# Moving two of the seven products: the fourth product of a Bu group goes up two places, and the first output group takes its second product before its fifth

## The chip, the cores and the metric

The kernel runs on one core of one Trainium2 chip. Its time is device microseconds from one execution of the whole program; a kernel is judged by the median of several executions. TensorE is called PE below, VectorE is DVE, ScalarE is ACT, GpSimd is POOL, and SyncE, which only issues transfers here, is SP.

## What is computed

The input x has 2048 rows (time) of 1024 columns. Two branches read it, and a gate per row mixes them:

```python
g = _sigmoid((x * gate_w).sum(-1, keepdims=True))
a = _A_ref(x, ...)        # Bu = x @ B_bar^T;  h[t] = Lam_bar * h[t-1] + Bu[t];  y = 2 Re(h @ C^T) + x * Dskip
b = _B_ref(x, ...)        # layernorm(x) -> @ w1 + b1 -> gelu -> @ w2 + b2
return g * a + (1 - g) * b
```

Branch a is a linear recurrence with 1024 complex states, branch b an MLP with 3584 hidden columns. Everything comes and goes in bf16.

## The kernel before, in words

**The matrix products.** Nearly all are done in groups of a 2 by 2 block product with seven multiplications instead of eight (Strassen in Winograd's form). Class `SG` writes one group: the methods `p1` to `p7` each put one accumulated product of 128 by 512 on PE (function `mm`, line 869 for the first product in a PSUM bank and line 871 for those that add to what stands there). A group uses three of the eight banks. Bank a gets p1, ACT copies it to bank b (the "seed", line 904), then p2 adds to a, and quadrant 0 is read out of a (`fin(0)`). Bank e gets p5, ACT saves it ("s5", line 888), then p3 adds to it and quadrant 1 is read out (`fin(1)`). Bank b starts with the seed; p6 adds to it and ACT saves it ("su", line 888 or 889); p7 adds, quadrant 3 is read out (`fin(3)`); p4 adds, quadrant 2 is read out (`fin(2)`). So p4 may start only when the read of quadrant 3 is over, p3 only after s5, p6 and p2 only after the seed.

**The stages**, in the order of PE: transposes and eight plain products; 14 groups of Bu (`bu_group`, four matmuls a product); then blocks of MLP groups, first layer (`m_group`, four matmuls a product) and second layer (`b_group`, seven), four of each, alternating; then eight output groups (`y_group`, eight matmuls a product). The second layer of half 1 adds its results to a DRAM buffer scr_ac by accumulating transfers from POOL's queue (line 1414); the output stage loads them back (line 1479). The recurrence itself (`ssm`: scans of line 1212, products of lines 1198 and 1201) runs on DVE beside all of this, at the lowest priority.

**The order of PE** is written out by hand: `mm` makes each product depend on the one before it. In a Bu group it is p1, p7 of the group before, p5, p6, p2, p3, p4 of the group before. At the passage from the last second-layer group (called b1.3 below) to the first output group (y0) it is p7 of b1.3, p1 of y0, p5 of y0, p4 of b1.3, p6, p2, p3 of y0, then p1 of y1 and so on.

**The order of the other engines** comes from a list planner (`Graph._schedule_once`): it plays the program through with costs that are constants of the file, and whenever an engine falls free it gives it the ready operation with the smallest priority; among equal priorities the one that was created first. Waits are then added, and each engine runs its list strictly in that order. A priority is a pair: a stage number and the running number of a product, less or more a few places.

**What reads out a Bu group.** `fin(0)` and `fin(2)` are ACT copies (line 1010) into a buffer that POOL stores to scr_u (line 947; there are two such buffers, used in turn by the groups). `fin(1)` is an add on DVE (line 1016). `fin(3)` is a copy by ACT into one small buffer uc (line 1019), of which there is one, and then an add on DVE (line 1021); only the copy must be over before p4.

**What reads out b1.3.** `fin(3)` is a DVE operation of line 1405, with priority (10, number of p7 of b1.3, less 2). The sums that y0 needs come from `y_prep(0, ...)`, called one group earlier: four operations of line 932, ys1 to ys4, with priority (10, number at the call plus 4), which comes to the same number. ys4 of y0 writes 2 KB of which the last 1 KB lies beyond the area SQ, in the first slot of the area AO; in that slot stands a result of group b1.2 until its accumulating transfer has read it. ys4 of y0 is read by p3 of y0.

Of the kernel before, what the change touches and what calls it, by code (L numbers as in the profile page):

```python
# [43 lines left out]
def c_dve(N):  # L44
    return 0.09 + N / 960.0
# [374 lines left out]
def build(nc, A_x, A_Lambda_re, A_Lambda_im, A_B_re, A_B_im, A_C_re, A_C_im, A_log_dt, A_Dskip,  # L420
# [25 lines left out]
    with es:  # L446
# [5 lines left out]
        def sem(name, dram=False):  # L452
            nsem[0] += 1
            return SemC(es.enter_context(nc.semaphore(name)), name, dram)
# [512 lines left out]
        def b_sums(pt, q):  # L967
            def bv(i, dt=FP16):
                return AR.v(bqo(pt, i), [(1, 512)], dt)
            dve_tt("bs1_%d" % pt, q, bv(4), bv(2, BF16), bv(3, BF16), ALU.add, 512)  # L970
            dve_tt("bs2_%d" % pt, q, bv(5), bv(4), bv(0, BF16), ALU.subtract, 512)
            dve_tt("bs3_%d" % pt, q, bv(6), bv(0, BF16), bv(2, BF16), ALU.subtract, 512)
            dve_tt("bs4_%d" % pt, q, bv(2), bv(1, BF16), bv(5), ALU.subtract, 512)

        def x_sums(pr, q):
            def xv_(i, dt=FP16):
                return AR.v(xqo(pr, i), [(1, 2048)], dt)
            dve_tt("ut1_%d" % pr, q, xv_(4), xv_(2, BF16), xv_(0, BF16), ALU.subtract, 2048)
            dve_tt("ut2_%d" % pr, q, xv_(5), xv_(3, BF16), xv_(4), ALU.subtract, 2048)
            dve_tt("ut3_%d" % pr, q, xv_(6), xv_(3, BF16), xv_(2, BF16), ALU.subtract, 2048)  # L980

        def x_sum4(pr, q):
            xv2, xv1, xv5 = AR.v(xqo(pr, 2), [(1, 2048)], FP16), AR.v(xqo(pr, 1), [(1, 2048)]), AR.v(xqo(pr, 5), [(1, 2048)], FP16)
            dve_tt("ut4_%d" % pr, q, xv2, xv1, xv5, ALU.subtract, 2048)
# [92 lines left out]
        def z_gate():  # L1077

            xs = [[xt(dt, c) for c in range(NCH)] for dt in range(DT)]

            def em(e):
                ins = None
                for dt in range(DT):
                    for c in range(NCH):
                        ins = e.matmul(bass.AP(PS[7], 32 * c * 512, [[512, 2], [1, CH]]), V(GWC, 2 * dt, [(1, 2)]), xs[dt][c].ap, start=(dt == 0), stop=(dt == DT - 1))
                return ins
            seq[0] += 1
            t = g.add("pe", 1.8, (1.0, seq[0]), em, reads=xs + [b_gwc], writes=[b_ps[7]], name="z", extra=pe_last)
            pe_last[:] = [t]
            g.add("act", c_act(CH), (1.0, seq[0]), lambda e: e.activation(zr.ap, V(PS[7], 0, [(1, CH)]), AF.Copy),  # L1090
                  reads=[b_ps[7]], writes=[zr, b_ps[7]], name="ze")
# [17 lines left out]
        def bT_dma(pt):  # L1109
            for ri, ap in enumerate((A_B_re, A_B_im)):  # L1110
                o = AR.v(bqo(pt, 2 * ri), [(128, DT), (1, 128)])
                g.dma((0.3, pt, ri), lambda e, o=o, ap=ap, pt=pt: e.dma_start_transpose(out=o.ap, in_=ap[pt * 128:(pt + 1) * 128, :]), 128 * D * 2,
                      ssem("bT", 2 * pt + ri), writes=[o], name="bTd%d.%d" % (pt, ri), xpose=True)
# [11 lines left out]
        prev = None  # L1125
        for n, (pt, pr) in enumerate(order):
            if pt not in summed:
                b_sums(pt, seq[0] - 1)
                summed.add(pt)
            if (pt, pr) == (0, 1):  # L1130
                x_sums(1, seq[0])
                x_sum4(1, seq[0])
            cur = bu_group(pt, pr)
            cur.p1()
            if prev is not None:
                prev.p7()
            if n == 1:
                z_gate()
                z_move()
                x_sum4(0, seq[0])  # L1140
            cur.p5()
            cur.p6()
            cur.p2()
            cur.p3()
            if prev is not None:
                prev.p4()
                opt = order[n - 1][0]
                if order[n - 1][1] == 1 and opt < 3:
                    bT_dma(opt + 5)
            prev = cur  # L1150
            bu_mark.append(list(pe_last))
# [384 lines left out]
        def make(it):  # L1536
            bi, x = it
            kind, Fh, c = blocks[bi]
            if kind == "m":
                return m_group(Fh, c, x, JORD[(Fh, c) in ((0, 1), (1, 0))][x])  # L1540
            if kind == "y":
                return y_group(x)
            return b_group(Fh, c, x)

        def prep_s(it, q):
            bi, x = it
            s_prep(x, q)
# [6 lines left out]
        prev = bu_last  # L1554
        cur = None
        early5 = False
        for n, it in enumerate(flat):
            bi, x = it
            kind, Fh, c = blocks[bi]
            last_of_block = (n + 1 == len(flat)) or flat[n + 1][0] != bi  # L1560
            nit = None if n + 1 == len(flat) else flat[n + 1]
            if (kind, Fh, c, x) == ("b", 1, 0, 3):
                y_load(0)
                y_load(1)
            if (kind, x) == ("y", 0):
                y_load(2)
            if cur is None:
                cur = make(it)
                cur.p1()

            if prev is not None:
                prev.p7()
            if kind == "b" and x + 1 < 4:
                prep_s((bi, x + 1), seq[0] + 4)
            if kind == "b" and Fh == 1 and c == 0 and x == 3:
                y_prep(0, seq[0] + 4)
            if kind == "y":
                if x + 1 < 8:
                    y_prep(x + 1, seq[0] + 4)
            early2 = kind == "b" and x == 0  # L1580
            if early2:
                cur.p2()
            if not early5:
                cur.p5()
            early5 = False
            cur.p6()
            if not early2:
                cur.p2()
            if nit is None:
                cur.p7()  # L1590
            cur.p3()
            if prev is not None:
                prev.p4()
                if kind == "y" and 1 <= x and x + 2 < 8:
                    y_load(x + 2)
                if kind == "m":
                    w2_step(seq[0] + 19)
                if kind == "m" and x > 0:
                    w1_next(18)
            if n == 0:  # L1600
                def em_b2(e):
                    return [e.dma_start(out=v.ap, in_=bass.AP(B_b2.tensor, B_b2.offset + o, [[0, 128], [1, 512]])) for (v, o) in ((v_b2l, 0), (v_b2r, 512))]
                g.dma((40.0, 0), em_b2, 128 * 2048, sem("d_b2b"), writes=[v_b2l, v_b2r], name="b2b", ndma=2)
                g.add("dve", c_dve(512), (40.0, 1), lambda e: e.tensor_tensor(v_b2d.ap, v_b2r.ap, v_b2l.ap, ALU.subtract), reads=[v_b2l, v_b2r], writes=[v_b2d], name="b2d")
                for pg in range(PG):
                    for q in range(NQ):
                        ssm(pg, q)
            prev, cur = cur, pend
            pend = None
            if last_of_block:  # L1610
                if nit is None:
                    prev.p4()
                else:
                    nk = blocks[nit[0]][0]
                    if nk == "b":
                        prep = True
                        b0 = None

                        cur = make(nit)
                        prev.p7()  # L1620
                        cur.p1()
                        prev.p4()
                        w1_next(20)
                        prep_s(nit, seq[0])
                        pend = make((nit[0], nit[1] + 1))
                        pend.p1()
                    else:
                        cur = make(nit)
                        prev.p7()
                        cur.p1()  # L1630
                        cur.p5()
                        early5 = True
                        prev.p4()
                    prev = None
                if (kind, Fh, c) == ("m", 1, 0):
                    ct_load(seq[0] + 20)

                if kind == "m":
                    if (Fh, c) == (0, 0):
                        xn_load(1, seq[0] + 20)  # L1640
                    elif (Fh, c) == (1, 1):
                        xn_load(0, seq[0] + 20)
                elif (Fh, c) == (0, 1):
                    w2_load(1)
# [43 lines left out]
```

## Time and profile before

| | us |
|---|---|
| median of 3 runs (558.56 to 558.93) | 558.57 |
| the profiled execution | 558.57 |
| its span, first to last instruction | 556.8 |

What lies around the span, 1.8 us, is start and end of the program. The profile has no second core and no change of TensorE's clock (granted 1.00 throughout). A row of a timeline gives the start, the time from the first start to the last end, engine, line, operation, what it writes and reads, how many instructions are merged, and in brackets how long the engine stood idle before it and what released it. The times of a PE row contain the filling of the array at its end, so the distance between two starts is the better measure of a product.

### The profile page before, as it was taken

To read this page: it belongs to the slowest core of one execution; us is meant where nothing else is said; L and a number is where in the kernel's file an instruction comes from. 1 tells how busy PE (TensorE), PEld (TensorE's weight loads), DVE (VectorE), ACT (ScalarE), POOL (GpSimd) and SP (SyncE) were. 2 spreads that over 40 slices of the span, in tenths; PEclk is the share of its full clock that TensorE was granted. 3 is DMA by queue.
4 is the path that set the end of the run, shared out by engine and by line. 5 is a ranking of instruction groups with operands and counts; after the bars stand their busy time and mean duration, and the time that the engine had idled before them with its cause. 6 is when DMAs were issued, how large, how long until landed. Compare 5 with 4: busy or idle time off the path is not lost.

```text
span 556.8 us, 7435 instructions
## 1 busy us (share of the span) xinstructions
PE 548.0 (98%) x2610; PEld 248.5 (45%) x2610; DVE 511.8 (92%) x867; ACT 283.1 (51%) x477; POOL 92.1 (17%) x146
## 2 busy tenths in 40 slices
PE   8999999989999999999999999999999999999997
PEld 5544444434444444444444444444444444444443
DVE  4999999999999999999999999999999867988873
ACT  3968899647774347674246753246662322111110
POOL 0226636630001110011110000220000211001000
DMA  9998999799492345576546866787669999686521
GB/s 263 243 310 204 260 283 275 235 354 328 151 226 97 135 185 181 169 233 230 208 163 197 284 142 156 140 196 196 201 159 257 233 286 320 215 325 238 191 99 57
DMA packets 114911, 120.08 MB, mean 216 GB/s; under 512 B 70322, under 2 KB 92594, under 8 KB 113850
## 3 DMA queue, kind: packets, MB, share of 16 engines
q1 hardware_dynamic: 102256, 73.69, 48.0%
q0 software_dynamic: 12480, 45.90, 26.5%
q8 instruction: 20, 0.33, 0.2%
q14 instruction: 17, 0.14, 0.1%
q10 hardware_dynamic: 138, 0.02, 0.0%
HBM read 56.40 MB, written 47.46 MB: 187 GB/s over the span
## 4 chain that ended last, share of the span: by engine, by line
PE 80%; DVE 13%; issue 2%; DMA 2%; POOL 2%; ACT 0%; DVEq 0%; ACTq 0%; POOLq 0%
PE ps L871 59%; PE ps L869 19%; DVE ar L932 3%; DMA scr_ac<-ar 2%; DVE ar L1212 2%; DVE ar L1198 2%; DVE ar L1061 1%; DVE ar L1016 1%; DVE ar L1021 1%; PE ps L686 1%; DVE ar L1201 1%; POOL cst L1052 1%; DVE ar L1322 1%; POOL scr_u L947 1%; DVE ar L852 1%
## 5 line engine op out<-in xcount | busy, mean ns | idle before, releaser
L871 PE MATMUL ps<-ar 128*128 128x512 f16 (+1 forms) x1832 | 414.3, 379 | 4.3 <-ACT ps L904 2.4
L871 PEld LDWEIGHTS ps<-ar 128*128 128x128 f16 (+1 forms) x1832 | 178.2, 98 | 223.2 <-ACT ps L904 4.2
L869 PE MATMUL ps<-ar 128*128 128x512 bf16 (+1 forms) x640 | 156.9, 379 | 0.1
L932 DVE TENSOR_TENSOR ar<-ar 128x512 f16<-128x512 bf16 (+6 forms) x216 | 138.9, 684 | 6.4 <-DMA scr_ac<-ar 4.9
L869 PEld LDWEIGHTS ps<-ar 128*128 128x128 bf16 (+1 forms) x640 | 62.2, 98 | 74.9 <-issue 0.4
L1212 DVE TENSOR_TENSOR_SCAN ar<-cst,init,ar 128x256 bf16<-128x256 f32 x128 | 88.8, 735 | 0.5
L888 ACT ACTIVATE ar<-ps 128x512 f32<-128x512 f32 x100 | 58.6, 594 | 50.2 <-PE ps L869 36.8
L1198 DVE TENSOR_TENSOR ar<-ar 128x2048 bf16<-128x2048 bf16 x64 | 77.0, 1218 | 0.1
L904 ACT ACTIVATE ps<-ps 128x512 f32<-128x512 f32 x66 | 38.5, 584 | 66.5 <-PE ps L869 61.9
L1318 ACT ACTIVATE ar<-ps,cst 128x512 bf16<-128x512 f32 x56 | 38.4, 687 | 21.5 <-PE ps L871 20.9
L889 ACT ACTIVATE ar<-ps,cst 128x512 f32<-128x512 f32 x32 | 22.0, 688 | 45.0 <-PE ps L871 19.3
L1324 ACT ACTIVATE ar<-ar,cst 128x512 bf16<-128x512 f32 x56 | 40.0, 714 | 7.7 <-DVE ar L1322 7.5
L1201 DVE TENSOR_TENSOR ar<-ar 128x1024 bf16<-128x1024 bf16 x64 | 42.7, 685 | 0.3
L1402 ACT ACTIVATE ar<-ps,cst 128x512 f32<-128x512 f32 x32 | 22.0, 687 | 41.2 <-PE ps L871 41.2
L1322 DVE TENSOR_TENSOR ar<-ps,ar 128x512 f32<-128x512 f32 x56 | 38.2, 682 | 3.3 <-PE ps L871 3.0
L947 POOL DMA_DIRECT2D scr_u<-ar x32 | 24.7, 774 | 62.1 <-ACT ar L962 22.8
L1503 DVE SCALAR_TENSOR_TENSOR ar<-ps,cst,ar 128x512 bf16<-128x512 f32 x32 | 23.8, 748 | 11.7 <-PE ps L871 11.6
L1230 POOL DMA_DIRECT2D scr_h<-ar x16 | 9.0, 564 | 125.4 <-DVE ar L1201 125.2
L1414 POOL DMA_DIRECT2D scr_ac<-ar x16 | 13.8, 892 | 81.2 <-DVE ar L1405 37.9
L1405 DVE SCALAR_TENSOR_TENSOR ar<-ps,cst,ar 128x512 f32<-128x512 f32 x32 | 23.8, 742 | 3.5 <-PE ps L871 3.2
L1482 DVE SCALAR_TENSOR_TENSOR ar<-ar,cst 128x1024 f32<-128x1024 bf16 x16 | 20.3, 1279 | 0.0
L1412 POOL DMA_DIRECT2D scr_ac<-ar x16 | 8.5, 532 | 69.2 <-DVE ar L1405 28.0
(110 smaller groups left out, 241.9 us busy)
## 6 DMA issues: line engine op xcount, KB each, us to landing
scr_ac<-ar POOLq DMA_DIRECT2D x32, 512.0 KB, 5.2
ar<-in_A_x_dram SPq DMA_DIRECT2D x32, 256.0 KB, 5.6
scr_u<-ar POOLq DMA_DIRECT2D x32, 256.0 KB, 5.3
ar<-scr_u SPq DMA_DIRECT2D x16, 512.0 KB, 5.2
scr_h<-ar POOLq DMA_DIRECT2D x16, 512.0 KB, 5.8
ar<-scr_ac SPq DMA_DIRECT2D x16, 512.0 KB, 6.9
ar<-scr_h SPq DMA_DIRECT2D x8, 1024.0 KB, 6.7
ar<-in_B_w_dram SPq DMA_DIRECT2D x14, 512.0 KB, 6.5
```

The costliest lines, as they stand in the source:

```text
L869: ins = e.matmul(V(PS[bk], 0, [(1, n)]), st[i].ap, mv[i].ap, start=(i == 0), stop=(i == K - 1))
L871: ins = e.matmul(V(PS[bk], 0, [(1, n)]), st[i].ap, mv[i].ap, start=False, stop=(i == K - 1), skip_group_check=True)
L888: return e.activation(o.ap, V(PS[bk], 0, [(1, 512)]), AF.Copy)
L904: g.add("act", c_act(512), (pb[0], q - 2), lambda e: e.activation(V(PS[b], 0, [(1, 512)]), V(PS[a], 0, [(1, 512)]), AF.Copy), reads=[b_ps[ ...
L932: g.add("dve", c_tt16(n), (pb[0], q), lambda e: e.tensor_tensor(o.ap, a.ap, b.ap, op), reads=[a, b], writes=[o], name=nm).slack = slack
L947: g.dma((1.0, q), lambda e: e.dma_start(out=US[pt // 4, :, 4 * pr:4 * pr + 4, r0:r0 + T], in_=evv.ap), 2 * 128 * CH * 2, ssem("us", 2 * ks ...
L1198: g.add("dve", c_tt16(UE), pri(i), lambda e: e.tensor_tensor(o.ap, a.ap, tbl.ap, ALU.mult), reads=[a, tbl], writes=[o], name=nm + tag)
L1201: g.add("dve", c_tt16(UE // 2), pri(i), lambda e: e.tensor_tensor(o.ap, a.ap, b.ap, op), reads=[a, b], writes=[o], name=nm + tag)
L1212: lambda e, pt=pt, ri=ri, vin=vin, go=go: e.tensor_tensor_scan(go.ap, Cb("R", pt, T), vin.ap, V(INIT, pt * 2 + ri, [(1, 1)]), ALU.mult, AL ...
L1318: g.add("act", c_act(512, ap_operands=1), (10.0, q + 1), lambda e: e.activation(o.ap, V(PS[bk], 0, [(1, 512)]), AF.Gelu_apprx_tanh, bias=C ...
L1322: g.add("dve", c_dve(512), (10.0, q - 2), lambda e: e.tensor_tensor(sv.ap, V(PS[bk], 0, [(1, 512)]), sv.ap, ALU.add), reads=[b_ps[bk], sv] ...
L1324: g.add("act", c_act(512, psum=False, ap_operands=1), (10.0, q + 3), lambda e: e.activation(o.ap, sv.ap, AF.Gelu_apprx_tanh, bias=C("B1", ...
```

## The change

In a Bu group p4 of the group before moves up two places, ahead of p2 and p3 of the new group. At the passage to the output stage, p5 of y0 is no longer issued early; p4 of b1.3 follows p1 of y0 directly, and p2 of y0 comes next, then p5, p6 and p3. The number of operations and what they compute stay as they were.

```diff
@@ -1140,10 +1140,11 @@
                 x_sum4(0, seq[0])
             cur.p5()
             cur.p6()
+            if prev is not None:
+                prev.p4()
             cur.p2()
             cur.p3()
             if prev is not None:
-                prev.p4()
                 opt = order[n - 1][0]
                 if order[n - 1][1] == 1 and opt < 3:
                     bT_dma(opt + 5)
@@ -1577,7 +1578,7 @@
             if kind == "y":
                 if x + 1 < 8:
                     y_prep(x + 1, seq[0] + 4)
-            early2 = kind == "b" and x == 0
+            early2 = kind != "m" and x == 0
             if early2:
                 cur.p2()
             if not early5:
@@ -1624,6 +1625,11 @@
                         prep_s(nit, seq[0])
                         pend = make((nit[0], nit[1] + 1))
                         pend.p1()
+                    elif nk == "y":
+                        cur = make(nit)
+                        prev.p7()
+                        cur.p1()
+                        prev.p4()
                     else:
                         cur = make(nit)
                         prev.p7()
```

## Rows read from the trace of the kernel before

**Rows 1.** Page, head and part 1: busy time, share of the span, instructions.

```profile
span 556.8 us, 7435 instructions
PE 548.0 (98%) x2610; PEld 248.5 (45%) x2610; DVE 511.8 (92%) x867; ACT 283.1 (51%) x477; POOL 92.1 (17%) x146
```

**Rows 2.** Waits of PE, whole span: total us, times, longest.

```profile
PE ps L871 <- ACT ps L904: 2.4, 2, 2.1
...
PE ps L871 <- DVE ar L1405: 0.7, 1, 0.7
PE ps L871 <- ACT ar L888: 0.5, 1, 0.5
PE ps L871 <- DVE ar L1322: 0.5, 1, 0.5
```

**Rows 3.** Timeline of PE, last Bu and first MLP groups.

```profile
117.08 1.90 PE L871 MATMUL ps<-ar 128*128 128x512 bf16 x8 [0.52 <-ACT ar L888]
118.81 1.03 PE L869 MATMUL ps<-ar 128*128 128x512 bf16 x4
119.68 1.03 PE L871 MATMUL ps<-ar 128*128 128x512 f16 x4
...
123.71 3.63 PE L871 MATMUL ps<-ar 128*128 128x512 f16 x16 [2.14 <-ACT ps L904]
```

**Rows 4.** Timeline of ACT, same stretch.

```profile
115.94 0.60 ACT L1019 ACTIVATE ar<-ps 128x512 f32<-128x512 f32 x1 [2.15 <-DVE ar L1021]
...
122.45 0.72 ACT L1324 ACTIVATE ar<-ar,cst 128x512 bf16<-128x512 f32 x1 [2.84 <-DVE ar L1322]
123.08 0.58 ACT L904 ACTIVATE ps<-ps 128x512 f32<-128x512 f32 x1
```

**Rows 5.** Timeline of DVE, same stretch.

```profile
115.17 0.68 DVE L1021 TENSOR_TENSOR ar<-ar 128x512 bf16<-128x512 f32 x1
...
119.39 1.22 DVE L1198 TENSOR_TENSOR ar<-ar 128x2048 bf16<-128x2048 bf16 x1
120.53 0.69 DVE L1021 TENSOR_TENSOR ar<-ar 128x512 bf16<-128x512 f32 x1
121.13 0.68 DVE L1201 TENSOR_TENSOR ar<-ar 128x1024 bf16<-128x1024 bf16 x1
121.73 0.69 DVE L1322 TENSOR_TENSOR ar<-ps,ar 128x512 f32<-128x512 f32 x1
```

**Rows 6.** Timelines of PE and ACT in the Bu stage, around 72 us.

```profile
71.79 3.84 PE L871 MATMUL ps<-ar 128*128 128x512 f16 x16 [0.29 <-ACT ps L904]
...
72.59 0.60 ACT L1019 ACTIVATE ar<-ps 128x512 f32<-128x512 f32 x1
```

**Rows 7.** Timeline of PE at the passage to the output stage.

```profile
454.60 3.62 PE L869 MATMUL ps<-ar 128*128 128x512 bf16 x16
458.92 6.87 PE L871 MATMUL ps<-ar 128*128 128x512 f16 x31 [0.71 <-DVE ar L1405]
465.62 1.89 PE L869 MATMUL ps<-ar 128*128 128x512 bf16 x8
467.35 1.89 PE L871 MATMUL ps<-ar 128*128 128x512 f16 x8
```

**Rows 8.** Timeline of DVE at the passage to the output stage.

```profile
457.51 0.69 DVE L932 TENSOR_TENSOR ar<-ar 128x1024 f16<-128x1024 bf16 x1 [4.89 <-DMA scr_ac<-ar]
458.12 0.74 DVE L1405 SCALAR_TENSOR_TENSOR ar<-ps,cst,ar 128x512 f32<-128x512 f32 x1
```

**Rows 9.** The chain that ended last, in order of time: start, us, what.

```profile
444.30 13.19 DMA scr_ac<-ar
```

**Rows 10.** Line 1414, 420 to 465 us: the accumulating transfers' time to landing.

```profile
DMA to landing us min/median/max: 8.1/9.4/13.2
```

**Rows 11.** Windows: us, busy time of engines, granted clock, DMA share, GB/s.

```profile
124.00:126.00 2.00, 2.00 (x11) 0.92 (x10) 2.00 (x6) 0.90 (x3) 0.00 (x0) 1.00 0.69 181
```

**Rows 12.** Groups of PE by form, the first matmuls of the program: busy, mean ns, idle.

```profile
L686 PE MATMUL ps<-ident 128*128 128x512 bf16 x9 | 4.0, 631 | 1.4 <-POOL init L788 1.4
```

## Prediction, made blind

> **What bounds the kernel now.** I read the page's head first: PE is busy 548.0 of 556.8 us [rows 1]. Of the 8.8 us left, an order of products can win or lose only what stands in the waits of PE, 4.1 us [rows 2]: 2.4 for the seed copy, 0.7 for the read of quadrant 3 in the second layer, 0.5 for a saved product, 0.5 for an add of the first layer; the rest is the start and the tail. No more than these can be won, and no product gets shorter. So the question is in which of the two places a stall of PE is shortened, and in which one is made longer.
>
> The timeline places them. The first is the passage from Bu to the MLP: p3 of the first MLP group m0 starts 0.52 us late, and p6 of m1 2.14 us late [rows 3]. The reader is to follow this back. p6 of m1 waits for the seed, which ACT began at 123.08, behind a gelu (line 1324) for which ACT had stood idle 2.84 us [rows 4]; that gelu waited for the add of line 1322, which DVE began at 121.73 [rows 5]. The product p3 of m0 that this add reads was done two products (from 117.08) after its start plus the filling, near 118.1 us. In between DVE was not idle: it worked off products of the recurrence and u adds one after the other. So here the backlog of DVE sets PE's time, not PE's order. The 0.52 us come from the same engine: ACT waited 2.15 us for the add of line 1021 [rows 4], since uc has one buffer, and that add stood on DVE behind a row of scans and started at 115.17 [rows 5].
>
> The second place is the passage to the output stage. PE did p1 and p5 of y0 (16 matmuls from 454.60), then stood 0.71 us, then went on with p4 of b1.3 at 458.92 [rows 7]. p4 waited for quadrant 3 of b1.3, read by DVE from 458.12, and DVE did that right behind ys4 of y0, before which it had been idle for 4.89 us, on a transfer into scr_ac [rows 8]. That is the slot in AO: ys4 may not write until the accumulating transfer of b1.2 has read it. The chain of what ended last has this transfer in it with 13.19 us [rows 9], while the median of its kind nearby is 9.4 [rows 10].
>
> **Part 1: p4 two places up in 13 Bu groups.** No instruction is added. A product takes 0.87 us here (118.81 to 119.68, [rows 3]). p4 starts 2 x 0.87 = 1.73 us earlier, p2 and p3 each 0.87 later.
>
> What becomes tighter: between p7 and p4 there stay two products, 1.73 us, where there were four. In that time ACT must do the copy of line 1019, 0.60 us. For 11 of the 13 groups the copy's end in the trace lies before the end of the second product, so nothing is lost. For two it doesn't: at 72.59 the copy began [rows 6] and ended at 73.19, while p6 of the next group, from 71.79, ends 0.87 later, at 72.66. That is a stall of 0.55 us, and the other one (copy at 65.90) is as long. Together 1.1 us at most. I count them as nothing, since PE then still waits at 121.6 for DVE, whose backlog is independent of them: the cover is the 2.14 us stall. Without the cover they cost 1.1.
>
> What becomes looser: p3 has one product more between it and the saved s5. The stores of quadrant 2, behind p4, leave POOL up to 1.73 us earlier, and the buffer they free two groups later is the one that the add of line 1021 writes. The planner can then put this add ahead of one or two scans. So I expect the 2.15 us idle on ACT [rows 4] and the 0.52 us stall to go. But that alone wins nothing at the end: the 2.14 us stall behind it gets longer by as much, for its end is set by DVE's list. What moves the end is how many operations of the recurrence the planner puts ahead of the first add of line 1322. As its PE runs with fewer waits (s5, p3), this add becomes ready earlier in the plan, and at least one operation of line 1201 that stood just ahead of it (121.13) falls behind it. From 121.13 to 121.73 that is 0.60 us; with what the earlier line 1021 add gives, I take 0.68, the row's own length. Bounds: both stalls gone, -2.66; one operation of line 1198 more in front, 119.39 to 120.53, +1.14. I take the value near the middle because rows 5 have short operations next to the add and none of them is free to vanish.
>
> **Part 2: p4 of b1.3 follows p1 of y0.** A product of an output group takes 1.73 us (465.62 to 467.35, [rows 7]). p1 of y0 begins at 454.60 and ends at 456.33. In the kernel before p5 of y0 then filled PE until 458.2; now p4 is next on PE, and it waits for the read at 458.12 to 458.86 [rows 8]. Nothing that the change moves acts on that read: ys4 and the read of quadrant 3 have the same priority number, ys4 was created first, and both are queued before the first moved product. The transfer that holds ys4 up was issued at 444, ten microseconds before. So p4 starts at 458.92 as before and PE stands 458.92 - 456.33 = 2.59 us instead of (by the row) 0.71, or, by starts of products (454.60 + 2 x 1.73 = 458.06), 0.86. The difference is one product, 1.73 us: p5 has to be done after all, behind the stall. Queued behind the waiting p4 are p2, p5, p6 and p3 of y0 and all the rest; from there to the last product PE has no wait [rows 2], so nothing takes it up again. Cost +1.73. The other waits come out at nothing: p2 of y0 needs the seed, which ACT can do in the stall; s5 then has p6, 1.73 us, to be saved in, against a copy of 0.60; p3 needs ys4, done long before. The transfers that p4's end frees leave at the same time as before. Bounds: +1.73 if the read stays behind the transfer, -0.71 if it doesn't (rival below).
>
> The clock is one point more. In the trace PE stood 2.14 us [rows 3] and the granted clock right after was 1.00 [rows 11], so I put the stall of 2.59 at nothing beyond its length. [...]
>
> **Sum.** -0.68 + 1.73 = +1.05 us. The profiled execution took 558.57 us, the same as the median, so the forecast is 559.6.
>
> **The rivals.**
>
> *The read of b1.3 no longer waits for the transfer.* If DVE has the read of line 1405 ahead of ys4, it runs at once behind p7 (ready about 454.8, done 455.6), p4 starts at 456.33 without a stall, and the 0.71 us are won: 558.57 - 0.71 - 0.68 = 557.2, faster. It happens if in the new plan the transfer of b1.2 lands later than p7 of b1.3 ends, for then ys4 isn't ready and the read is taken first; or, in the run, if the transfer takes its median, 9.4 instead of 13.19 us, and lands near 453.7. For it: the planner's lists of DVE and POOL are made anew behind part 1, and a shift of an operation or two of the recurrence can move POOL's stores at 435 to 444. Against it: everything around this place hangs on PE's products in both plans alike, and the order of priorities favours ys4. Chance 0.28.
>
> *The passage to the MLP loses its stall altogether.* If the planner puts the seed of m1 ahead of the first gelu of line 1324 on ACT, p6 of m1 doesn't wait for DVE any more: -2.66 + 1.73 gives 557.6. For it: in [rows 4] the two stand directly next to each other. Against it: the add gets earlier in the plan, which keeps the gelu first. Chance 0.12.
>
> *Part 1 does nothing that counts* (DVE's list ahead of the add keeps its length, or the two short stalls of copies are not covered): 558.57 + 1.73 = 560.3, up to 561.4. Chance 0.16.
>
> *The longer stall lowers the clock.* The nine first matmuls of the program took 4.0 us [rows 12], 0.45 each; at 0.216, a quarter of 0.87, they would be 1.9, so a fall would add about 2 us: 561.7. [...] Chance 0.02.
>
> That the order doesn't change as the diff says can be left out: each product depends on the one before it by line 873.
>
> **How the numbers follow.** The likeliest case, 559.6, has 0.42; its own range is 558.9 to 560.4, by 0.5 us to each side for one short DVE operation more or less and 0.2 for the landing. The rivals have 0.28, 0.12, 0.16 and 0.02. I let the range reach to 556.8 below, past the case of 557.2, and to 560.8 above; left out are the ends of the rivals, about 0.2. A measurement of this kernel tells a change of some 0.2%, 1.1 us, from none. Faster (below 557.45): most of the first rival and a third of the second, 0.25. Slower (above 559.7): nearly half of the likeliest, the third and the fourth, 0.36. Within: 0.39.
>
> **What would show it.** After the change PE's timeline should have at the passage to the output stage eight matmuls of line 869, a stall near 2.6 us put down to line 1405, then 7 + 8 of line 871 and 8 of line 869; DVE should have its idle of 5 us before ys4 with line 1405 behind it. If instead line 1405 comes first, part 2 is wrong and the first rival right. At 115 to 124 the add of line 1021 should start some 2 us sooner after the scans, the 0.52 us stall be gone, and the wait for the seed end 0.6 us sooner on the program's clock. The two short stalls near 66 and 72 us should show, put down to line 1019. The prediction fails if new waits appear in the later blocks, since all lists of DVE are planned anew.

## The result, and the profile after

The changed kernel takes 562.87 us (median of 4, 562.40 to 563.47), the one before 558.57 (558.36 to 558.93): a ratio of 1.0077, with a 95% interval of 1.0059 to 1.0094. It is slower, on the side that was forecast, but by 4.3 us instead of 1.05, and outside the range. The profiled execution took 563.18 us with a span of 561.5.

The head of the page and the waits of PE, to be read against [rows 1, 2] (total us, times, longest):

```profile
span 561.5 us, 7405 instructions
PE 545.7 (97%) x2562; PEld 249.2 (44%) x2610; DVE 511.0 (91%) x867; ACT 284.4 (51%) x477; POOL 91.2 (16%) x146
```

```profile
PE ps L871 <- ACT ps L904: 3.7, 2, 2.6
PE ps L871 <- DVE ar L1406: 2.4, 1, 2.4
...
PE ps L871 <- DVE ar L1323: 1.1, 2, 0.8
PE ps L871 <- DVE ar L932: 1.1, 1, 1.1
```

Lines behind the edits have moved by a few: 1406 and 1323 are the 1405 and 1322 of before, 1605 is 1604. There is a wait that the kernel before didn't have at all (line 932), the seed waits longer, the read of quadrant 3 much longer. PE's timeline has them one by one, against [rows 3, 7]:

```profile
36.76 2.76 PE L871 MATMUL ps<-ar 128*128 128x512 f16 x11 [1.08 <-DVE ar L932]
...
121.75 3.63 PE L871 MATMUL ps<-ar 128*128 128x512 f16 x15 [1.07 <-ACT ps L904]
...
130.62 3.63 PE L871 MATMUL ps<-ar 128*128 128x512 f16 x16 [2.65 <-ACT ps L904]
...
460.15 5.09 PE L871 MATMUL ps<-ar 128*128 128x512 f16 x15 [2.44 <-DVE ar L1406]
465.08 1.89 PE L869 MATMUL ps<-ar 128*128 128x512 f16 x8
...
471.98 1.89 PE L871 MATMUL ps<-ar 128*128 128x512 f16 x8
```

Starts of the same product in both traces show where the time goes:

| product | before | after | difference |
|---|---|---|---|
| p6 of MLP group m1 | 123.71 | 121.75 | -1.96 |
| p6 of the next one, m4 | 129.76 | 130.62 | +0.86 |
| p4 of b1.3 | 458.92 | 460.15 | +1.23 |
| p7 of y0 | 467.35 | 471.98 | +4.63 |
| span | 556.8 | 561.5 | +4.7 |

So PE is 2.0 us ahead by p6 of m1, more than forecast, loses 2.8 in the group after that, and 3.4 go at the passage to the output stage. The 0.4 between m4 and that passage is mostly a new wait of 0.38 us for line 1323 near 161 us.

The gain comes from DVE, whose first add of m0 (line 1322, now 1323) starts at 119.78 instead of 121.73 [rows 5]. First a row near 57 us from the kernel before, then two rows after (timelines of DVE):

```profile
56.98 1.46 DVE L1061 TENSOR_SCALAR ar<-ar,cst 128x1024 bf16<-128x1024 bf16 x3 [0.47 <-POOL cst L1056]
```

```profile
111.22 0.67 DVE L1021 TENSOR_TENSOR ar<-ar 128x512 bf16<-128x512 f32 x1
119.78 0.68 DVE L1323 TENSOR_TENSOR ar<-ps,ar 128x512 f32<-128x512 f32 x1
```

The loss in m4 is read back from the seed. DVE and ACT after, and the subtraction in the kernel before (timelines):

```profile
123.62 1.22 DVE L1199 TENSOR_TENSOR ar<-ar 128x2048 bf16<-128x2048 bf16 x1
128.03 0.69 DVE L1605 TENSOR_TENSOR ar<-ar 128x512 f32<-128x512 bf16 x1 [3.19 <-DMA ar<-in_B_b_dram]
128.64 0.68 DVE L1323 TENSOR_TENSOR ar<-ps,ar 128x512 f32<-128x512 f32 x1
```

```profile
129.36 0.72 ACT L1325 ACTIVATE ar<-ar,cst 128x512 bf16<-128x512 f32 x1 [3.25 <-DVE ar L1323]
129.98 0.58 ACT L904 ACTIVATE ps<-ps 128x512 f32<-128x512 f32 x1
```

```profile
128.88 0.69 DVE L1604 TENSOR_TENSOR ar<-ar 128x512 f32<-128x512 bf16 x1 [0.38 <-DMA ar<-in_B_b_dram]
```

Line 1605 subtracts the two halves of the bias b2, once in the program; its result is first used some 25 us later, by ACT at 154.12. It has to wait for a load in two parts of 128 KB, and in the new list of DVE it stands ahead of the first add of m1 (the row of line 1323 at 128.64). So DVE, which had been the busy engine, stood idle for 3.19 us; the add, the gelu and the seed came late one behind the other. In the kernel before the second part of the load was issued at 121.7 instead of 117.9 and the subtraction stood behind that add; it waited 0.38 us there, and PE didn't wait for it.

At the passage to the output stage DVE did just what [rows 8] show, 1.2 us later, and the clock did something new. Timeline of DVE, the transfer in the chain that ended last, then windows (us, busy PE, PEld, DVE, ACT, POOL, granted clock, DMA share, GB/s):

```profile
458.74 0.69 DVE L932 TENSOR_TENSOR ar<-ar 128x1024 f16<-128x1024 bf16 x1 [4.90 <-DMA scr_ac<-ar]
459.35 0.75 DVE L1406 SCALAR_TENSOR_TENSOR ar<-ps,cst,ar 128x512 f32<-128x512 f32 x1
```

```profile
445.53 13.19 DMA scr_ac<-ar
```

```profile
460.00:462.00 2.00, 1.85 (x5) 0.74 (x6) 1.90 (x4) 0.00 (x0) 0.00 (x0) 0.54 1.03 268
462.00:464.00 2.00, 2.00 (x8) 0.68 (x5) 0.00 (x0) 0.58 (x1) 0.00 (x0) 0.61 1.08 277
464.00:466.00 2.00, 2.00 (x11) 0.94 (x10) 0.72 (x2) 0.11 (x1) 0.86 (x1) 1.00 1.01 272
```

The 15 matmuls of p4 and of p2 of y0 took 465.08 - 460.15 = 4.93 us. At the 0.216 us of the others they take 3.24. That is 1.69 us for a clock that was granted at 0.54 and 0.61 in the windows from 460 and 462, right behind the stall, and at 1.00 from 464. With the product of 1.73 us that had to be done behind the stall it makes the 3.4 us.

### The profile page after: what moved, and what is told of

It is laid out like the page before. It is cut to its first block, busy times and chain, and to the rows that moved or that the text cites. A ratio compares the mean times of both kernels' runs of the same rounds, so it can differ in the third digit from the quotient of the medians.

```text
span 561.5 us, 7405 instructions
## 1 busy us (share of the span) xinstructions
PE 545.7 (97%) x2562; PEld 249.2 (44%) x2610; DVE 511.0 (91%) x867; ACT 284.4 (51%) x477; POOL 91.2 (16%) x146
## 4 chain that ended last, share of the span: by engine, by line
PE 73%; DVE 17%; DMA 4%; issue 2%; POOL 2%; ACT 2%; SPq 0%; DVEq 0%; ACTq 0%; POOLq 0%
PE ps L871 56%; PE ps L869 16%; DVE ar L932 6%; DMA scr_ac<-ar 2%; DVE ar L1213 2%; DVE ar L1323 2%; DMA ar<-in_B_b_dram 2%; DVE ar L1199 2%; DVE ar L809 1%; DVE ar L1202 1%; PE ps L686 1%; DVE ar L1016 1%; ACT ar L674 1%; DVE ar L1061 1%; POOL cst L1055 0%
## 5 line engine op out<-in xcount | busy, mean ns | idle before, releaser
L871 PE MATMUL ps<-ar 128*128 128x512 f16 (+1 forms) x1799 | 413.9, 380 | 10.1 <-ACT ps L904 3.7
L869 PE MATMUL ps<-ar 128*128 128x512 bf16 (+1 forms) x625 | 154.5, 379 | 1.3 <-DVE ar L658 0.6
```

What stands on the lines that cost most here:

```text
L869: ins = e.matmul(V(PS[bk], 0, [(1, n)]), st[i].ap, mv[i].ap, start=(i == 0), stop=(i == K - 1))
L871: ins = e.matmul(V(PS[bk], 0, [(1, n)]), st[i].ap, mv[i].ap, start=False, stop=(i == K - 1), skip_group_check=True)
```

## The experiments

All times are medians. The kernel before ran beside each batch on the same chip: 559.2 us on all three chips, 86 executions. Its median lies 0.6 above the first one because it has two levels: 54 executions with a mean granted clock of 0.999 or 1.000, at 558.8 us, and 32 at 0.996 or 0.997, at 560.4. In what follows "full clock" means the first kind. The second kind is read as one fall of the clock, worth 1.6 us by these two medians, and 0.994 as two: every trace at 0.996 or 0.997 has one stretch in which 15 or 16 matmuls took 4.9 to 5.2 us instead of 3.2 to 3.5 (where windows of 2 us were read there, the lowest granted clock was 0.50 to 0.56), the two at 0.994 (e2, e6) have two, those at 1.000 none.

**e1: the Bu part alone** (the first hunk of the diff, on the kernel before).

> The kernel before with the Bu part of the change alone. Theory: the loss has two independent places. At the passage to the output stage the changed kernel lost 1.73 us of stall (0.71 to 2.44) and about 1.7 us of matmuls at a lowered clock; both go away here, so 562.87 - 3.4 = 559.4 us, still slower than before by about 0.9, with the stalls of the Bu part unchanged: 1.1 us near 37 us, 1.1 near 122, 2.65 near 130 us. Rival: the Bu part alone is a gain or nothing, as predicted (557.9 to 558.6), and everything lost belongs to the passage.

559.28 us, ratio 1.0002 (0.9987 to 1.0017); at full clock 559.11 in 11 of 12 executions against 558.77, so 0.3 us slower. PE's stalls are those of the changed kernel (1.10, 1.08, then 1.73 for the seed of m4), and 0.74 at the passage to the output stage, so the stalls of the two places don't depend on each other. The theory's 0.9 was too much: the second part of the bias load took 9.2 us from its issue instead of 10.1 in the first trace, and the stall at m4 was 1.73 us instead of 2.65. The rival's "nothing" is nearly right for the sum, though not for its parts.

**e2: the passage to the output stage alone** (the other two hunks, on the kernel before).

> The kernel before with the part at the passage to the output stage alone. Theory: p4 of the last second-layer group waits for the same read as before, behind the transfer, so the stall grows by one product, 0.71 to 2.44 us: 558.57 + 1.73 = 560.3 us if the clock stays, and about 562.0 if a stall of this length at this place lowers the clock as in the changed kernel. Rival: the stall in the changed kernel came from the shifted lists of the other engines, and alone this part costs nothing: 558.6.

564.28 us in seven executions (561.57 to 574.32), ratio 1.0081 (1.0049 to 1.0113). Four have one fall of the clock, at 562.02, near 558.77 + 1.73 + 1.6 (three of them at 561.6 to 562.3, one at 566.08). The profiled one, 564.28, had two falls, one behind the 2.14 us stall near 123 (granted 0.58 and 0.56 in the windows from 124 and 126) and one at the passage (0.50 in the one from 463), and a transfer that was later still (DVE waited 5.77 us for it):

```profile
461.23 5.10 PE L871 MATMUL ps<-ar 128*128 128x512 f16 x15 [3.31 <-DVE ar L1405]
```

The theory holds; the rival falls, for in the trace DVE and ACT do the same operations in the same order as in the kernel before up to this read. Why three executions took 566.08, 567.81 and 574.32 us stays open.

**e3: the bias subtraction later.**

```diff
-                g.add("dve", c_dve(512), (40.0, 1), lambda e: e.tensor_tensor(v_b2d.ap, v_b2r.ap, v_b2l.ap, ALU.subtract), reads=[v_b2l, v_b2r], writes=[v_b2d], name="b2d")
+                g.add("dve", c_dve(512), (40.0, 1), lambda e: e.tensor_tensor(v_b2d.ap, v_b2r.ap, v_b2l.ap, ALU.subtract), reads=[v_b2l, v_b2r], writes=[v_b2d], name="b2d").slack = 4.0
```

> The changed kernel, with one operation planned later: the DVE subtraction of the bias (line 1605), which waits for a load, gets 4 us of slack in the planner and so stands behind the adds of MLP group m1. Theory: the 2.65 us stall of PE near 130 us is the wait for this load, carried on from DVE over an add and a gelu to the seed: it goes, and the time is 562.87 - 2.65 = 560.2 us. Rival: it is the general backlog of DVE, and the stall only moves to another group: 562.5 to 562.9.

558.78 us. The wait for the seed is down to the one of 1.07 us (waits of PE of this kernel):

```profile
PE ps L871 <- DVE ar L1406: 2.4, 1, 2.4
...
PE ps L871 <- ACT ps L904: 1.1, 1, 1.1
```

So the stall at m4 was the wait for the load, and the backlog didn't take its place. More came back than the 2.65 us because one fall of the clock less is in the median: at full clock it is 558.49 in 8 of 12, against 561.1 of the changed kernel at full clock (e5, on another chip), -2.6. That is still more than the 1.90 us that this stall had in e5's trace; the rest of up to 0.7 us is not accounted for. The stall at the passage to the output stage is still there, but behind it the 15 matmuls took 3.41 us, not 5.09, and the clock stayed up, granted 1.00 in the windows from 455 to 467 (PE's timeline):

```profile
456.91 3.41 PE L871 MATMUL ps<-ar 128*128 128x512 f16 x15 [2.45 <-DVE ar L1406]
```

So that stall by itself doesn't bring the fall each time.

**e4: ys4 of y0 behind the read of quadrant 3.**

```diff
-            dve_tt("ys4_%d" % yi, q, ysq(yi, 3), hk(yi, 1, 0), ysq(yi, 1), ALU.subtract, 1024)
+            dve_tt("ys4_%d" % yi, q, ysq(yi, 3), hk(yi, 1, 0), ysq(yi, 1), ALU.subtract, 1024, 3.0 if yi == 0 else 0.0)
```

> The changed kernel, with the fourth sum of output group y0 (ys4) planned 3 us later, so that DVE does the read of quadrant 3 of the last second-layer group first. Theory: p4 of that group no longer waits for the accumulating transfer, the 2.44 us stall goes, and the clock is not lowered: 562.87 - 2.44 - 1.7 = 558.7 us. Rival: DVE's wait for the transfer holds up something else instead (p3 of y0, which needs ys4), and no more than 1 us comes back: 562.

558.98 us. PE goes through the passage without a stall (p1 of y0, p4 and p2, p5):

```profile
455.57 1.67 PE L869 MATMUL ps<-ar 128*128 128x512 bf16 x7
457.08 3.40 PE L871 MATMUL ps<-ar 128*128 128x512 f16 x15
460.32 1.89 PE L869 MATMUL ps<-ar 128*128 128x512 f16 x8
```

15 matmuls from 457.08 take 3.24 us to the next start, and 11 of 12 executions have full clock. Theory held, to 0.3 us. The trace has a new stall of 0.87 us further on, at 490.70, for a load of scr_h.

**e5: the changed kernel again.**

> The changed kernel once more, beside the others on one chip. The Bu part alone gave the time of before here, and mending the bias wait took 4 us off the whole change, more than the 2.65 us of the stall. Theory: the rest is the clock: a stall of over 2 us is followed in some executions by some 3.4 us at half the clock, 1.7 us lost each time, and this kernel has two such stalls. Then its times lie in steps of about 1.7 us: 561.1 with no fall, 562.8 with one, 564.5 with two, and the mean granted clock goes 1.000, 0.997, 0.994 with them. Rival: the changed kernel is 562.9 us in every execution and the steps are no more than noise.

562.51 us in 12 executions, ratio 1.0049 (1.0030 to 1.0068): two at 561.1 with a mean clock of 1.000, eight at 562.5 with 0.997 (one of them has 561.2), two at 564.75 with 0.994 (561.0 to 565.0 in all). The steps are there. All four executions of the first measurement were at 0.997, one fall each. Of the four of the kernel before beside them none took over 558.93 us, so by their times they had none.

**e6: the first of the 13 moves taken back.**

```diff
-            if prev is not None:
+            if prev is not None and n > 1:
                 prev.p4()
             cur.p2()
             cur.p3()
+            if n == 1:
+                prev.p4()
```

> The changed kernel with the first of the 13 moves taken back (p4 of the first Bu group stays behind p3, where its sum is ready). Theory: the 1.1 us stall near 37 us goes, but PE then comes 1.1 us sooner to the passage to the MLP, where DVE's backlog sets the time; the 1.1 us stall there grows to about 2.1 and the time stays: 0 to -0.3 us against the changed kernel. Rival: the stall near 37 us is lost time of its own: -1.1 us.

563.46 us, six of seven executions with two falls. The timeline shows the first half of the theory, and what it had left out:

```profile
122.06 1.26 PE L871 MATMUL ps<-ar 128*128 128x512 f16 x4 [2.31 <-ACT ps L904]
...
130.68 3.63 PE L871 MATMUL ps<-ar 128*128 128x512 f16 x16 [0.72 <-ACT ps L904]
```

The 1.08 us stall near 37 is gone, and the one at m1 has grown by 1.2 to 2.31; p6 of m1 starts at 122.06, no sooner than in e5 (121.83): what is won ahead of DVE's backlog is lost at it. The longer stall was now followed by a granted clock of 0.68 and 0.50 in the windows from 122 and 124, but that fall is covered by the wait for the bias load, which shrank from 1.90 us in e5 to 0.72. p6 of m4 starts 0.72 us later than in e5 (129.96), and DVE's subtraction just as much (128.09 against 127.37), since the load landed later in this trace. The rival falls, and so does the theory's zero: 0.9 us slower. Why the load was later is not shown. The seventh execution took 567.18 us at 0.997.

**e7: the parts that help, without the two that hurt** (Bu part without its first move, both slacks of e3 and e4, passage as before).

> The Bu part without its first move, the bias subtraction planned 4 us later, ys4 of y0 planned 3 us later, and the passage to the output stage as before. Theory: no stall near 37, 130 and 459 us is left, only those at DVE's backlog near 122 (2.1 us) and the add near 330; against the kernel before the 0.71 us at the passage and some 2 us of the 2.14 + 0.52 us at 117 to 124 are won, with the planner's 0.9 us: 558.6 - 2.5 = 556.1 us. Rival: what is won near 122 us is given back at the next group, as in the changed kernel: 558.

556.68 us, ratio 0.9951 (0.9930 to 0.9972); 556.53 at full clock. One larger stall is left, 2.86 us for the seed of m1; four of the ten executions had a fall. Theory right, 0.4 to 0.6 us short of it.

**e8: ys4 behind the read, on the kernel before.**

> The kernel before with ys4 of y0 planned 3 us later, nothing else. Theory: DVE reads quadrant 3 at once, p4 of the last second-layer group has no stall, and 0.71 us are won: -0.7 us against the kernel before. Rival: p3 of y0, which needs ys4 behind the late transfer, waits instead: 0.

558.10 us, ratio 0.9980 (0.9953 to 1.0008), which alone doesn't settle it; at full clock 557.87 in 9 of 12 against 558.73. No stall at the passage in the trace: DVE read quadrant 3 at 454.96 and waited 1.97 us for the transfer only behind it. PE doesn't wait at p3 either, so ys4 is there in time. Two of the other three executions were far off (564.49 and 569.73 us); why is open.

**e9: e7 with a gelu planned later.**

```diff
-                          reads=[sv, bc("B1")], writes=[o], name="gelu" + nm)
+                          reads=[sv, bc("B1")], writes=[o], name="gelu" + nm).slack = 2.5 if (jj, c, qd) == (0, 0, 1) else 0.0
```

> The faster version of e7 with one gelu more planned later (the first one of line 1324 gets 2.5 us of slack, so that ACT copies the seed and the saved product of group m1 ahead of it). Theory: the 2.9 us stall at 122 us is no lack of DVE but a seed queued behind this gelu on ACT; it goes, and with it the last stall after which the clock fell: 554 to 554.5 us, and no execution with a mean clock under 0.999. Rival: DVE's backlog sets the time there; the next products wait for it instead, and no more than 0.5 us is won: 556.2.

555.71 us, ratio 0.9922 (0.9889 to 0.9955), 10 of 11 executions at full clock. The waits of PE:

```profile
PE ps L871 <- DVE ar L1325: 2.3, 3, 1.1
PE ps L686 <- POOL init L788: 1.4, 1, 1.4
```

The seed no longer waits, so its place on ACT was part of the stall. But 1.14 us come back at 123.38, where p4 of m0 waits for the add of quadrant 3: the rest was DVE. Between theory and rival, 1.2 us short of the forecast. The theory's "no execution under 0.999" missed by one, at 0.997 and 563.63 us. It is the fastest version.

**e10: e7 with the passage of the change** (the other two hunks).

> The version of e7, but with the passage to the output stage as the change has it (p4 of the last second-layer group right behind p1 of y0). Theory: that order costs only where the read of quadrant 3 is late; with ys4 planned behind the read it costs nothing: the same as e7, 556.7 us within 0.3. Rival: the order has a cost of its own (the seed or the saved product of y0 comes too late for p2 or p3): +0.5 us or more.

557.29 us, ratio 0.9939 (0.9913 to 0.9966), on another chip; at full clock 556.18 against 556.53 of e7. PE has no stall at the passage. The medians alone differ by 0.6 us, the rival's price, but they hold falls in 5 of 12 and 4 of 10 executions, and the intervals of the two ratios overlap. So no cost of the order itself is seen; it is the late read that makes it cost. Of the five falls here, the profiled execution's stands behind the stall of 2.02 us at 121.02:

```profile
122.00:124.00 2.00, 2.00 (x6) 0.76 (x5) 2.00 (x5) 1.20 (x2) 0.00 (x0) 0.50 0.91 314
```

**e11: the opposite edit**, p1, p5 and p2 of y0 ahead of p4 of b1.3, on the kernel before.

```diff
-            if not early2:
+            if not early2 and (kind, x) != ("y", 0):
                 cur.p2()
...
                         early5 = True
+                        if nk == "y":
+                            cur.p2()
                         prev.p4()
```

> The kernel before with the opposite edit at the passage: p1, p5 and p2 of y0, and only then p4 of the last second-layer group. Theory: the read is late by a fixed time, so one product more in front of p4 covers the 0.71 us: -0.7 us against the kernel before. Rival: p4 waits as it did, since the transfer that holds up DVE comes later still: 0.

559.08 us, ratio 0.9987 (0.9963 to 1.0011): by the medians no difference. At full clock 557.98 in 6 of 12 against 558.88, and the trace has no stall there although DVE waited 4.84 us for the transfer as ever. With one fall it is 559.18 in 5 against 560.20 in 11. So the theory's 0.7 us are there at either level, under the falls of the clock, of which this measurement had more (6 of 12 against 11 of 28). The profiled execution had one, behind the 2.14 us stall at 123.71 that the kernel before has too (windows):

```profile
124.00:126.00 2.00, 2.00 (x6) 0.73 (x5) 2.00 (x6) 0.54 (x2) 0.00 (x0) 0.50 0.72 209
```

## Why the prediction was right or wrong

**Part 2, the passage to the output stage: the mechanism and the size of the stall were right.** Predicted +1.73 us, one product done behind the stall; the stall went from 0.71 to 2.44, by 1.73. The read stayed behind ys4 and the transfer, 13.19 us in both chains. The first rival (the read goes first) didn't come by itself; e4 and e8 brought it about by hand, and it is worth what was put down, 0.7 to 0.9 us.

**The clock was the step that failed there.** "I put the stall of 2.59 at nothing beyond its length", from one row, the granted clock of 1.00 behind the 2.14 us stall. One execution was taken for the rule. By the mean clock, 32 of 86 executions of the kernel before have a fall themselves, and in the traces of e2 and e11, where that stall is the same, it stands right behind it. The rival's price, "about 2 us", was the author's estimate; that the clock is what made the first matmuls of the program slow, from which it is worked out, no run shows (granted 1.00 in each window of 1 us from 0 to 10 of the kernel before). In its place the runs showed 1.6 by the levels and 1.69 by the row. Its chance of 0.02 was wrong: the changed kernel had at least one fall in all of its first four executions and in 10 of 12 later, in both traces at the passage. What makes it so frequent there stays open: with such a stall (2.45 us) but without the bias wait (e3) only 4 of 12 had one.

**Part 1, the passage to the MLP: the forecast step came, but most of the gain there was luck.** Predicted -0.68; p6 of m1 came 1.96 us sooner, in spite of a new stall of 1.08 before it. The add of line 1021 stood ahead of two scans and started at 111.22 instead of 115.17, the 0.52 us stall is gone, and one operation of line 1201 fell behind the first add of line 1322, as forecast: 6 of them ran ahead of it instead of 7, 4.00 us instead of 4.68. Nothing else left DVE's list ahead of that add. Most of the other 1.3 us have causes that the prediction didn't name: DVE's wait of 0.47 us for POOL near 57 us is gone, and its sixteen operations of line 1061 took 8.27 us in all instead of 8.88. Why those became shorter was not tried. The forecast's 0.68 was also a value picked within wide bounds; the row that it rests on gives 0.60. And p3 of m0, which it puts "two products" behind 117.08, is one product long there; the 118.1 us that it goes on with are right. That stalls ahead of DVE's backlog cost nothing was right too; e6 shows it.

**What failed in part 1 was that the gain was carried to the end of the program.** The prediction had said that it would fail "if new waits appear in the later blocks, since all lists of DVE are planned anew", but gave this no term and no price. The wait that appeared is the bias subtraction: 2.65 us at p6 of m4 in the first trace, 1.73 to 1.90 in those of e1, e4 and e5; e3, which takes it away, gets 2.6 back. With it part 1 is +0.3 (e1) instead of -0.68. Without it, by e3 less the 1.73 us of the passage that e3 keeps, it would be about -2.0 (an estimate, at full clock), as large as the gain at p6 of m1.

**A need of the moved step itself was overlooked.** p4 of the first Bu group reads a sum (ut4) that DVE makes only after the gate's product has read the same place. Two places earlier p4 is there before it: 1.08 us. It cost nothing in the end, but only because of the cover. The two stalls at the copies near 66 and 72, which were forecast, didn't come. PE was there about 1 us later, behind that new stall, but they are missing in e6 too, which doesn't have it: the copies themselves began sooner there, at 64.53 and 70.62 instead of 65.90 and 72.59.

**The sum.** At full clock the changed kernel is at 561.1 (two executions) against 558.7, +2.4; the parts make 1.73 + 0.3 = 2.0. Of the rest up to 4.3, 1.6 us are the clock: the first measurement set executions with one fall against executions that, by their times, had none. That leaves 0.3 us, and 0.4 between the parts and the whole, which are not accounted for. The bias wait, longer by 0.75 us in the first trace than in e5's, would be enough, but no other execution of the first measurement has a trace.

## What to carry to other kernels

Moving a step in a kernel whose other queues come from a planner is two edits: the one in the diff, and a new list on every engine. Look in the new lists for operations that wait for a load and stand ahead of the critical chain; holding one such operation back was worth more here than any order of products. A product that waits for a read should be as late as its bank allows when that read hangs on a transfer, and a stall need not be over when the wait ends: behind the one of 2.44 us the granted clock was 0.54 and 0.61 in the two windows from 460 to 464.

## What the runs showed of the hardware that was not expected

In the traces the granted clock fell, to 0.50 to 0.56 at the lowest where windows were read, behind stalls of 2.0 to 3.3 us between long busy stretches, but not each time: in the first trace of the changed kernel not behind 2.65 us at 130.62 but behind 2.44 us at 460.15, and in e3's not behind 2.45 us. Counted by the mean clock and grouped after the fact, kernels with one stall of that kind have falls in part of their executions: 32 of 86 with 2.14 us, 3 and 6 of 12 with the same in e8 and e11, 5 of 12 with 2.02 (e10), 4 of 12 with 2.45 (e3), 4 of 10 with 2.86 (e7). Where two stalls of 1.9 us or more stand in the trace (the changed kernel, e2, e6) it is 27 of 30. Where, behind the start, none is over 1.9 us (e1, e4, e9), it is 3 of 35. So the length of the stall alone doesn't decide; what else does is left open.

The two 128 KB parts of the bias load took 6.8 and 10.1 us from issue to landing in the changed kernel, against 5.3 and 7.2 us in the kernel before, though they were issued 3.8 us sooner; the subtraction began at 128.03 and 128.88. The stretch from 112 to 130 us moved 345 GB/s on the mean (338 before); which transfer held the load up was not tried.
